# First expert weights in pairs, a last batch joined in halves, and inner blocks in two transfers

## The chip, the cores and the metric

The kernel runs on one core of one Trainium2 chip. The metric is the device time of one execution in microseconds (us), lower is better; the time given is the median of several executions. Beside it stands one execution recorded by the hardware profiler, from which all rows below come.

The engines are called as in the profile: PE is the matrix engine (PEld its weight loads), DVE the vector engine, ACT the scalar engine, POOL the third elementwise engine, SP the engine that issues nearly all transfers (DMAs) between memory and the on-chip buffer. PSUM banks, eight of them, take the results of matmuls.

## What is computed

Three stages follow one another: attention with a window of 64 positions over 4 batches, 8 heads, 576 positions and 64 values per head; a soft mixture of 8 experts with 4 slots each; and a feed-forward layer with a gated activation.

```python
scores = q @ k.T / 8, masked to 0 <= i - j < 64          # per batch and head
x = softmax(scores) @ v                                   # then (2304, 512)
logits = x @ phi                                          # (2304, 32)
d = exp(logits - logits.max(0)); d /= d.sum(0) + 1e-9     # over all tokens
slot_input = d.T @ x                                      # (32, 512)
for e in range(8):                                        # 4 slots each
    slot_out[e] = relu(slot_input[e] @ w1[e]) @ w2[e]     # 512x1024, 1024x512
c = softmax(logits, axis=1); x = c @ slot_out
h = x @ w_in; out = (h / (1 + exp(-1.702 * h))) @ w_out   # 512x2048, 2048x512
```

`w_in` and `w_out` come in 64-bit floats and are narrowed on the chip; everything else is 32-bit.

## The kernel before

**Attention steps.** The loop over `i` in `range(ns)` has 18 steps: 16 units (a batch and a pair of heads) and two that collect the last 64 positions of the batches. In each step PE makes scores (`emit_s`, L331 and L346), transposes the probabilities of the step before (`emit_t`, L366), transposes finished outputs (`xt_step`, L419) and makes the products with the values (`emit_pv`, L381). All engines run this in the order in which the code is written; the schedule is by hand (`manual_schedule`). SP issues the queries and keys of step `i + 3` (`load_qk`, L244), the values of step `i + 2` (`load_v`, L258) and, by the table `W_AT`, some weights (`load_w`, L154 and L164): at steps 10 to 15 (`AHEAD`) before the values, at the others behind them. SP waits at each issue until the buffer is free, and for the oldest of eight transfers under way, so its queue is in order.

**Weights.** Each expert's first and second weights come in slices of 1 MB, 128 rows of 2048 numbers. `w1` has 16 slices, one transfer each; `w2` has 16 too, of which 14 already come in pairs of 2 MB (`w2p`, L154), one alone, and the last in three pieces (`PIECES`, L164). `plan` lists them in order: the 16 of `w1`, then those of `w2`; each `load_w(1)` takes the next. Eight buffers of a pair each hold them, and the first `w2` go to parts of the `arena` that the attention has left. Four blocks of `w_in` (`early_load`, L169) are loaded in the first two steps, 512 KB each, into `raws`.

**The running sum of the slots.** `slot_input` is summed batch by batch with a running maximum: `acc` holds the sum so far in four groups of 32 rows, `al` is the factor by which it shrinks when the maximum moves. `gather` does `acc = acc * al + psl` for batches 1 and 2. For batch 3 (the last) and the 64 last positions of every batch (the "tail") this happens behind the loop, in the join: `psl` (L510) is the product of batch 3, `pl` (L760) that of the tail, whose rows 0 to 63 hold columns 0 to 255 and rows 64 to 127 columns 256 to 511 (`HALVES`). ACT scales `acc` by `al3`, the product of both factors (L764); DVE adds `psl * al` (L772) and then `pl`, half by half (L782). PE multiplies by `i4s` (L784), which sums the four row groups and divides by the sum of exponentials; ACT and DVE copy the two halves of the result `psi`, which lie in one bank, to `siT` (L786). PE then runs the experts: `emit_w1` (L810, four rounds), `emit_w2` (L853, 14 slices), `next_w2` (L912) and `last_w2` (L920).

**Feed-forward.** The rest, from about 135 us, loops over 48 blocks (L1065) and loads blocks of `w_out` and `w_in` while it runs. The change doesn't touch its code, but for the place of the `w_in` blocks in memory.

Of the kernel before, what the change touches and what calls it, by code (L numbers as in the profile page):

```python
# [10 lines left out]
F32 = mybir.dt.float32  # L11
# [5 lines left out]
ALU = mybir.AluOpType  # L17
# [14 lines left out]
HALVES = (slice(0, 256), slice(256, 512))  # L32
LAST_CUT = (slice(0, 384), slice(384, 512))
PIECES = (slice(0, 2), slice(2, 3), slice(3, 4))
W_AT = {**{i: 1 for i in range(2, 17)}, 12: 0, 15: 2, 16: 2, 17: 1}
L_AT = 12
AHEAD = range(10, 16)

# [29 lines left out]
FP = 4  # L68

@with_exitstack  # L70
def attention_softmoe_ffn(
# [6 lines left out]
    w1: bass.AP,  # L78
    w2p: bass.AP,
    w2s: bass.AP,  # L80
    w_in: bass.AP,
    w_out: bass.AP,
    out: bass.AP,
# [56 lines left out]
        return mem(2048 * i, 2048).rearrange("p (a f) -> p a f", a=4)  # L140

    w1t, w2t = [], []
    plan = [(w1t, w1, i, None if i < N_E else i - N_E) for i in range(16)]
    plan += [(w2t, w2p, i, i if i < 7 else None) for i in (0, 2, 4, 6, 7, 9, 11, 13, 15)]
    plan.reverse()

    def load_w(n=1):
        for _ in range(n):
            if plan:
                lst, src, i, d = plan.pop()  # L150
                if src is w2p and i not in (6, 15):
                    t = wpair() if d is None else mem(2048 * d, 4096).rearrange(
                        "p (n a f) -> p n a f", n=2, a=4)
                    nc.sync.dma_start(  # L154
                        out=t.rearrange("p n a f -> p (n a f)"), in_=w2p[W2P.index(i)])
                    lst.extend([t[:, 0], t[:, 1]])
                    continue
                t = wslot() if d is None else dslot(d)
                v = (w2s[i // 15] if src is w2p else src[i]).rearrange("p (a f) -> p a f", a=4)
                if not plan:  # L160
                    t, v = [x.rearrange("p a f -> p (a f)").rearrange(
                        "p (c a f) -> p c a f", c=4, a=4) for x in (t, v)]
                for c in PIECES if not plan else (slice(0, 4),):
                    nc.sync.dma_start(out=t[:, c], in_=v[:, c])  # L164
                lst.append(t)


    def raw_load(raw, src):
        nc.sync.dma_start(out=raw.bitcast(I32), in_=src.bitcast(I32))  # L169
# [32 lines left out]
    def early_dst(n):  # L202
        return win_dst(n) if n < FP else wof[:, n - FP, :]

    def early_raw(n):
        return raws[n // 2].rearrange("p a f -> p (a f)")[:, 1024 * (n % 2):1024 * (n % 2) + 1024]

    def early_load(n):
        src = w_in[n] if n < FP else w_out[n - FP]
        if wide:  # L210
            raw_load(early_raw(n), src)
        else:
            nc.sync.dma_start(out=early_dst(n), in_=src)


    qkb = [rawt[:, 0:1024]] + [mem(QK0 + 1024 * i, 1024) for i in range(2)]
# [519 lines left out]
    nc.vector.tensor_tensor(out=al, in0=m, in1=run["m"], op=ALU.subtract)  # L736
    psl = slots()
    load_w(1)
    sides[0][0]()
    ss = sp.tile([128, 1], F32, tag="ss", name="ss")  # L740
    nc.scalar.activation(
# [6 lines left out]
        nc.tensor.transpose(pd[:, t, :], ltt[0:32, t * 128:t * 128 + 128], ident[0:32, 0:32])  # L748
    sr = sp.tile([128, 1], F32, tag="srun", name="srun")
    nc.vector.tensor_tensor(out=sr, in0=run["s"], in1=al, op=ALU.mult)  # L750
    al3 = sp.tile([128, 1], F32, tag="al3", name="al3")
    nc.vector.tensor_tensor(out=al3, in0=run["al"], in1=al, op=ALU.mult)
    nc.vector.tensor_copy(dt, pd)
    pm = bank("m")
    nc.tensor.matmul(pm[:, 0:1], i4m, sr, start=True, stop=True)
# [1 line left out]
    for c in range(2):  # L757
# [3 lines left out]
                pl[32 * g:32 * g + 32, HALVES[c]], dt[:, t, :], xl[:, t, HALVES[c]],  # L761
                start=True, stop=True, tile_position=(0, 32 * g))
    load_w(1)
    nc.scalar.activation(out=acc, in_=acc, func=ACTF.Copy, scale=al3)  # L764
    rsl = sp.tile([128, 1], F32, tag="rsl", name="rsl")
    nc.vector.tensor_scalar(
        out=rsl, in0=pm[:, 0:1], scalar1=ss, scalar2=1e-9, op0=ALU.add, op1=ALU.add)
# [1 line left out]
    i4s = cst.tile([128, NS], F32, name="i4s")  # L769
    nc.vector.tensor_scalar(  # L770
        out=i4s, in0=i4m[:, 0:NS], scalar1=rsl, scalar2=None, op0=ALU.mult)
    nc.vector.scalar_tensor_tensor(  # L772
        out=acc, in0=psl, scalar=al, in1=acc, op0=ALU.mult, op1=ALU.add)
    siT = phis
    sides[1][0]()
    for k in range(2):
        sides[k][1]()
    sides[2][0]()
    psi = bank("m", (128, KD, 32))
    for k, c in enumerate(HALVES):  # L780
        p = slice(64 * k, 64 * k + 64)
        nc.vector.tensor_tensor(out=acc[p, c], in0=pl[p, c], in1=acc[p, c], op=ALU.add)  # L782
        for kk in (2 * k, 2 * k + 1):
            nc.tensor.matmul(  # L784
                psi[:, kk, :], acc[:, kk * 128:kk * 128 + 128], i4s, start=True, stop=True)
        (nc.vector.tensor_copy if k else nc.scalar.copy)(  # L786
            siT[:, 2 * k:2 * k + 2], psi[:, 2 * k:2 * k + 2])
    sides[2][1]()
    ht = rawt
    nc.gpsimd.memset(ht[:, 0:LS0], 0.0)  # L790
# [99 lines left out]
    def win_more():  # L890
        n = FP + len(iraw)
        if n == NF:
            return
        if n % FP == 0:
            winf.append(gp.tile([128, 4, 512], F32, tag="wi", name="wi", bufs=2))
        iraw[n] = gp.tile([128, 1024], F32, tag="iraw", name="iraw", bufs=2)
        if wide:
            raw_load(iraw[n], w_in[n])
        else:
            nc.sync.dma_start(out=win_dst(n), in_=w_in[n])  # L900

    so = hsb[0]
    soT = rawt[:, 0:512].rearrange("p (k s) -> p k s", k=KD)
# [295 lines left out]
def _layout(q, k, v, moe_phi, moe_w1, moe_w2, moe2_w_in, moe2_w_out):  # L1199
    def units(a):  # L1200
        return a.reshape(B, NHP, 2, S, D)

    def words(a):
        return a.view(np.int64) if a.dtype == np.float64 else a

    order = np.concatenate(
        [np.arange(c * CH, c * CH + CH) for c in list(range(0, 8, 2)) + list(range(1, 8, 2))])
    qf = units(q).transpose(0, 1, 2, 4, 3).reshape(NU, 128, S)
    kf = units(k).transpose(0, 1, 2, 4, 3).reshape(NU, 128, S)
    vf = units(v).transpose(0, 1, 3, 2, 4).reshape(NU, S, 128)  # L1210
    qk = np.concatenate([qf[:, :, 0:512], kf[:, :, order]], axis=2)
    vt = vf[:, 0:512].reshape(NU, 4, 128, 128).transpose(0, 2, 1, 3)
    o7, e8 = slice(448, 512), slice(512, 576)
    sq = np.concatenate([qf[:, :, e8], kf[:, :, e8], kf[:, :, o7]], axis=2)
    sq = sq.reshape(B, NHP, 128, 192).transpose(0, 2, 1, 3).reshape(B, 128, 768)
    sv = np.concatenate([vf[:, e8], vf[:, o7]], axis=1)
    vt = np.concatenate([vt, sv.reshape(B, NHP, 128, 128).transpose(0, 2, 1, 3)], axis=0)
    one = np.zeros(vt.shape[:3] + (1,), vt.dtype)
    vt = np.concatenate([vt, one], axis=3).reshape(NU + B, 128, 516)
    vt = np.concatenate([one[:, :, 0], vt], axis=2)  # L1220
    ph = moe_phi.reshape(KD, 128, NS).transpose(1, 0, 2).reshape(128, KD * NS)
    w1 = moe_w1.reshape(2, 4, 4, 128, 2, 512).transpose(0, 4, 2, 3, 1, 5).reshape(16, 128, 2048)
    w2 = moe_w2.reshape(8, 2, 4, 128, 512).transpose(0, 1, 3, 2, 4).reshape(16, 128, 2048)
    last = w2[15:].reshape(1, 128, 4, 4, 128).transpose(0, 1, 3, 2, 4).reshape(1, 128, 2048)
    w2p = np.stack([np.concatenate([w2[i], w2[i + 1]], axis=1) for i in W2P])
    w2s = np.stack([w2[6], last[0]])
    wi = moe2_w_in.reshape(4, 128, 4, 512).transpose(2, 0, 1, 3).reshape(16, 128, 512)
    wo = moe2_w_out.reshape(16, 128, 512)
    return {"qk": qk, "vt": vt, "sq": sq, "phi": ph, "w1": w1, "w2p": w2p, "w2s": w2s,
            "w_in": words(np.ascontiguousarray(wi)), "w_out": words(np.ascontiguousarray(wo))}  # L1230


# [22 lines left out]
```

## Time and profile before

| | us |
|---|---|
| median of 3 executions | 362.58 (362.48 to 362.71) |
| the profiled execution | 362.39 |
| its span | 360.6 |
| PE busy in it | 351.1 (97%) |
| PE weight loads busy | 270.0 (75%) |
| DVE busy | 242.0 (67%) |
| ACT busy | 195.3 (54%) |

The span runs from the first to the last instruction; the time of the execution has a little more around it. The granted PE clock is at full speed in all 40 slices of the page. A chain of waits is followed back from the last instruction: each piece is work or a transfer that the next one waited for, and "issue" is time in which an engine waited for nothing that the profile shows. A transfer has a time of issue and a time from issue to landing; transfers that wait behind others show it in the second.

### The profile page before, as it was taken

Reading aid. Unit: us, or ns where it says so; the run is one execution under the profiler, and the core shown is the slowest. Engines: PE = TensorE matmul, PEld = TensorE weight load, DVE = VectorE, ACT = ScalarE, POOL = GpSimd, SP = SyncE. Lnnn points to the kernel's source line nnn. Section 1 sums busy time; section 2 is a strip of 40 time slices with the busy share of each in tenths; the row PEclk is TensorE's granted clock in tenths of the full one; section 3 lists DMA queues with packets and bytes.
Section 4 is the critical chain, followed back from the end, with each engine's and each line's share of the span. In section 5 each row is a group of like instructions: output and inputs, shape, how many; then the busy total and the mean of one; then the engine's idle time right before and its main releaser. Section 6 shows DMA issues by size and latency. Waiting matters only on the chain.

```text
span 360.6 us, 7721 instructions
## 1 busy us (share of the span) xinstructions
PE 351.1 (97%) x3021; PEld 270.0 (75%) x3021; DVE 242.0 (67%) x527; ACT 195.3 (54%) x499; POOL 45.4 (13%) x90
## 2 busy tenths in 40 slices
PE   7999999998999999999999999999999999999995
PEld 6787787776634357888788887788886888888884
DVE  3767797986626328885867695988687876262624
ACT  2898899777314027765657444554445453333330
POOL 4366764630100000000000000000000000000000
PEclk9999999999999999999999999999999999999999
DMA  7999999999999994333131313040300000040404
GB/s 275 410 414 403 410 410 412 400 400 411 413 423 429 421 399 136 109 123 111 60 116 55 121 58 117 32 143 2 116 2 0 0 2 1 0 176 0 175 2 175
DMA packets 17172, 70.87 MB, mean 197 GB/s; under 512 B 1904, under 2 KB 2288, under 8 KB 14064
## 3 DMA queue, kind: packets, MB, share of 16 engines
q1 hardware_dynamic: 16992, 70.18, 50.3%
q8 instruction: 24, 0.39, 0.5%
q10 hardware_dynamic: 144, 0.20, 0.2%
q14 instruction: 12, 0.10, 0.1%
HBM read 65.65 MB, written 4.72 MB: 195 GB/s over the span
## 4 chain that ended last, share of the span: by engine, by line
PE 93%; DVE 3%; ACT 1%; issue 1%; DMA 1%; DVEq 0%; ACTq 0%
PE s L1065 18%; PE t L1065 18%; PE v L1065 18%; PE v L381 5%; PE m L1033 5%; PE s L346 5%; PE m L366 4%; PE s L810 4%; PE v L853 3%; PE s L331 2%; PE m L419 2%; PE m L460 1%; PE m L510 1%; DVE nm L351 1%; DMA rawt<-in_qk_dram 1%
## 5 line engine op out<-in xcount | busy, mean ns | idle before, releaser
L1021 ACT ACTIVATE r<-m 128x384 fp32r<-128x384 f32 (+1 forms) x97 | 47.4, 491 | 80.7 <-PE m L1033 80.6
L1046 DVE TENSOR_TENSOR r<-g,r 128x384 fp32r<-128x384 f32 x96 | 51.4, 554 | 48.4 <-ACT g L1021 39.9
L1065 PE MATMUL t<-w,r 128*128 128x512 f32 x288 | 75.9, 395 | 0.0
L1065 PE MATMUL s<-w,r 128*128 128x512 f32 x288 | 74.3, 393 | 0.0
L1065 PE MATMUL v<-w,r 128*128 128x512 f32 (+2 forms) x291 | 73.4, 387 | 0.0
L1065 PEld LDWEIGHTS t<-w,r 128*128 128x128 f32 x288 | 53.8, 188 | 14.8 <-issue 4.0
L1065 PEld LDWEIGHTS v<-w,r 128*128 128x128 f32 x291 | 54.5, 188 | 11.3
L1065 PEld LDWEIGHTS s<-w,r 128*128 128x128 f32 x288 | 52.6, 188 | 8.5
L1021 ACT ACTIVATE g<-m 128x384 f32<-128x384 f32 x96 | 47.8, 500 | 0.0
L358 ACT ACTIVATE pa<-s,nm 128x128 f32<-128x128 f32 x140 | 40.9, 404 | 5.7 <-DVE nm L351 5.7
L351 DVE TENSOR_REDUCE nm<-s 128x4 f32<-128x512 f32 x35 | 22.5, 684 | 5.4 <-PE s L346 4.9
L1033 PE MATMUL m<-cT,w 128*128 128x384 f32 (+2 forms) x113 | 25.9, 320 | 0.0
L1033 PEld LDWEIGHTS m<-cT,w 128*128 128x128 f32 x113 | 20.8, 188 | 4.9 <-ACT g L1021 0.7
L366 PE MATMUL m<-ident,pa 128*128 128x128 f32 x144 | 20.9, 283 | 0.4 <-issue 0.2
L366 PEld LDWEIGHTS m<-ident,pa 128*128 128x128 f32 x144 | 15.6, 140 | 4.6 <-issue 1.7
L367 ACT COPY pa<-m 128x512 f32<-128x512 f32 x18 | 10.7, 596 | 10.3 <-PE m L366 10.3
L1001 ACT CAST w<-wf 128x512 fp32r<-128x512 f32 x15 | 9.4, 623 | 9.3 <-DVE wf L194 9.3
L810 PE MATMUL s<-w,phis 128*32 128x512 f32 x128 | 14.1, 594 | 0.0
L346 PE MATMUL s<-arena 64*64 64x128 f32 x352 | 13.8, 271 | 0.3 <-DVE arena L254 0.2
L400 DVE TENSOR_TENSOR arena<-v,rs 128x256 f32<-128x256 f32 x36 | 13.6, 419 | 0.6
L1004 DVE TENSOR_TENSOR w<-wf,w 128x512 fp32r<-128x512 f32 x15 | 10.3, 689 | 5.2 <-ACT w L1001 5.1
L1085 DVE TENSOR_TENSOR w<-s,w 128x512 f32<-128x512 f32 x18 | 11.6, 684 | 2.8 <-PE s L1065 2.8
(218 smaller groups left out, 454.4 us busy)
## 6 DMA issues: line engine op xcount, KB each, us to landing
w<-in_w_dram SPq DMA_DIRECT2D x16, 1024.0 KB, 9.4
w<-in_w_out_dram SPq DMA_DIRECT2D x16, 512.0 KB, 3.4
w<-in_w2p_dram SPq DMA_DIRECT2D x4, 2048.0 KB, 16.2
arena<-in_w2p_dram SPq DMA_DIRECT2D x3, 2048.0 KB, 10.5
iraw<-in_w_in_dram SPq DMA_DIRECT2D x12, 512.0 KB, 3.3
arena<-in_qk_dram SPq DMA_DIRECT2D x10, 512.0 KB, 9.0
out_dram<-w SPq DMA_DIRECT2D x16, 256.0 KB, 2.1
arena<-in_vt_dram SPq DMA_DIRECT2D x13, 258.5 KB, 7.3
```

Of the source, the lines that this page charges most:

```text
L346: nc.tensor.matmul(st[h][rows[j], c, :], q, k, start=False, stop=(c == 3), tile_position=(64 * h, 64 * j))
L351: nc.vector.tensor_reduce(out=nm[:, h], in_=st[h], axis=AX.X, op=ALU.max, negate=True)
L358: nc.scalar.activation(out=pb[h][:, c, :], in_=st[h][:, c, :], func=ACTF.Exp, bias=nm[:, h, c:c + 1], scale=1.0)
L366: nc.tensor.transpose(tt[:, c, :], pb[h][:, c, :], ident)
L381: nc.tensor.matmul(pvt[i][h][64 * j:64 * j + 64, c, :], ab[h][:, c, 64 * j:64 * j + 64], v, start=True, stop=True, tile_position=(0, 64 * j))
L400: nc.vector.tensor_tensor(out=o, in0=pv[h][:, :, 1 - h:65 - h], in1=rs[:, h].unsqueeze(2).to_broadcast([128, 4, 64]), op=ALU.mult)
L810: nc.tensor.matmul(ph[32 * j:32 * j + 32, :], siT[:, kk, :], w1t[4 * r + kk][:, j, :], start=(kk == 0), stop=(kk == KD - 1), tile_position ...
L1021: nc.scalar.activation(out=(gh, g)[part][:, a:e], in_=ph[:, a:e], func=ACTF.Gelu_apprx_sigmoid)
L1033: nc.tensor.matmul(ph[:, c - a:e - a], mst[:, f * 128:f * 128 + 128], cT(c, e - c), start=True, stop=True)
L1046: nc.vector.tensor_tensor(out=gl, in0=g, in1=gh.bitcast(F32), op=ALU.subtract)
L1065: nc.tensor.matmul(accs[t][:, h], a[:, c], b[:, h], start=(first and k == 0), stop=(last and k == 2 and h.stop == 512))
L1085: nc.vector.tensor_tensor(out=o[:, h], in0=accs[t][:, h], in1=o[:, h], op=ALU.add)
```

## The change

Four edits:

- `w1` is laid out in pairs of slices, as `w2` is, so that each transfer brings 2 MB, 128 rows of 4096 numbers. `W_AT` now names nine steps: a pair at 3, 5, 7, 9, 11, 14, 15, 16 and 17 (the one at 17 is the first of `w2`).
- The four inner blocks of `w_in` that are loaded early come in two transfers of 1 MB (`w_two`).
- In the join, `acc * al + psl` of batch 3 is done like that of the batches before, in two halves of the columns (`join`), as soon as `psl` is there. Behind it ACT scales only those quarters of `acc` to which DVE doesn't add the tail, and DVE scales the others as it adds (`acc * al + pl`). `al3` is gone.
- The two halves of `psi` lie in banks of their own.

```diff
-W_AT = {**{i: 1 for i in range(2, 17)}, 12: 0, 15: 2, 16: 2, 17: 1}
+W_AT = {i: 1 for i in (3, 5, 7, 9, 11, 14, 15, 16, 17)}
...
-    plan = [(w1t, w1, i, None if i < N_E else i - N_E) for i in range(16)]
+    plan = [(w1t, w1, i, None) for i in range(0, 16, 2)]
...
-                if src is w2p and i not in (6, 15):
+                if src is w1 or i not in (6, 15):
...
-                        out=t.rearrange("p n a f -> p (n a f)"), in_=w2p[W2P.index(i)])
+                        out=t.rearrange("p n a f -> p (n a f)"), in_=w1[i // 2] if src is w1 else w2p[W2P.index(i)])
...
     def early_load(n):
-        src = w_in[n] if n < FP else w_out[n - FP]
+        if n < FP:
+            if n % 2:
+                return
+            src = w_two[n // 2]
+            raw, o = raws[n // 2], winf[0][:, n:n + 2]
+            raw, o = [x.rearrange("p a f -> p (a f)") for x in (raw, o)]
+        else:
+            src, raw, o = w_out[n - FP], early_raw(n), early_dst(n)
...
     psl = slots()
     load_w(1)
+
+    def join(c):
+        nc.vector.scalar_tensor_tensor(
+            out=acc[:, c], in0=acc[:, c], scalar=run["al"], in1=psl[:, c], op0=ALU.mult, op1=ALU.add)
+
+    join(HALVES[0])
     sides[0][0]()
...
     nc.vector.tensor_tensor(out=sr, in0=run["s"], in1=al, op=ALU.mult)
-    al3 = sp.tile([128, 1], F32, tag="al3", name="al3")
-    nc.vector.tensor_tensor(out=al3, in0=run["al"], in1=al, op=ALU.mult)
+    join(HALVES[1])
     nc.vector.tensor_copy(dt, pd)
...
-    nc.scalar.activation(out=acc, in_=acc, func=ACTF.Copy, scale=al3)
+    for k, c in enumerate(HALVES):
+        q = slice(64 - 64 * k, 128 - 64 * k)
+        nc.scalar.activation(out=acc[q, c], in_=acc[q, c], func=ACTF.Copy, scale=al[q])
...
-    nc.vector.scalar_tensor_tensor(
-        out=acc, in0=psl, scalar=al, in1=acc, op0=ALU.mult, op1=ALU.add)
...
-    psi = bank("m", (128, KD, 32))
+    psi = [bank("m")[:, 0:64].rearrange("p (k s) -> p k s", k=2) for _ in range(2)]
     for k, c in enumerate(HALVES):
         p = slice(64 * k, 64 * k + 64)
-        nc.vector.tensor_tensor(out=acc[p, c], in0=pl[p, c], in1=acc[p, c], op=ALU.add)
+        nc.vector.scalar_tensor_tensor(
+            out=acc[p, c], in0=acc[p, c], scalar=al[p], in1=pl[p, c], op0=ALU.mult, op1=ALU.add)
         for kk in (2 * k, 2 * k + 1):
             nc.tensor.matmul(
-                psi[:, kk, :], acc[:, kk * 128:kk * 128 + 128], i4s, start=True, stop=True)
+                psi[k][:, kk % 2], acc[:, kk * 128:kk * 128 + 128], i4s, start=True, stop=True)
         (nc.vector.tensor_copy if k else nc.scalar.copy)(
-            siT[:, 2 * k:2 * k + 2], psi[:, 2 * k:2 * k + 2])
+            siT[:, 2 * k:2 * k + 2], psi[k])
```

What stands in SP's queue from the end of step 1 to step 5 (`in_qk` the queries and keys, `in_vt` the values, `in_w` the first weights), before:

```order
L244 DMA arena<-in_qk_dram 128x1024
L258 DMA arena<-in_vt_dram 128x517
L164 DMA w<-in_w_dram 128x2048
L244 DMA rawt<-in_qk_dram 128x1024
L258 DMA arena<-in_vt_dram 128x517
L164 DMA w<-in_w_dram 128x2048
L244 DMA arena<-in_qk_dram 128x1024
L258 DMA rawt<-in_vt_dram 128x517
L164 DMA w<-in_w_dram 128x2048
```

and after:

```order
L252 DMA arena<-in_qk_dram 128x1024
L266 DMA arena<-in_vt_dram 128x517
L252 DMA rawt<-in_qk_dram 128x1024
L266 DMA arena<-in_vt_dram 128x517
L155 DMA w<-in_w_dram 128x4096
L252 DMA arena<-in_qk_dram 128x1024
L266 DMA rawt<-in_vt_dram 128x517
```

Each weight transfer of an even step has gone, and that of the odd step behind it is twice as long.

DVE in the join, from the difference of the maxima (`al`) to the second half of the sum, before (`m` and `v` are the banks of `psl` and `pl`, `srun` the sum of exponentials):

```order
L736 TENSOR_TENSOR al<-mrun 128x1
L750 TENSOR_TENSOR srun<-srun,al 128x1
L752 TENSOR_TENSOR al_1880<-al 128x1
L753 COPY rawt<-m 128x64
L766 TENSOR_SCALAR rsl<-m,ss 128x1
L768 RECIPROCAL rsl<-rsl 128x1
L770 TENSOR_SCALAR i4s<-i_82,rsl 128x32
L772 SCALAR_TENSOR_TENSOR acc<-m,al,acc 128x512
L782 TENSOR_TENSOR acc<-v,acc 64x256 x2
```

and after:

```order
L744 TENSOR_TENSOR al<-mrun 128x1
L749 SCALAR_TENSOR_TENSOR acc<-acc,al,m 128x256
L764 TENSOR_TENSOR srun<-srun,al 128x1
L749 SCALAR_TENSOR_TENSOR acc<-acc,al,m 128x256
L766 COPY rawt<-m 128x64
L781 TENSOR_SCALAR rsl<-m,ss 128x1
L783 RECIPROCAL rsl<-rsl 128x1
L785 TENSOR_SCALAR i4s<-i_82,rsl 128x32
L795 SCALAR_TENSOR_TENSOR acc<-acc,al,v 64x256 x2
```

The update of 512 columns behind `i4s` has become two of 256 columns, ahead of the copy of `pd` (L753 before, L766 after).

## Rows read from the trace of the kernel before

**Rows 1.** The page: DMA engines' load in 40 slices; instruction queue, packets and MB.
```profile
DMA  7999999999999994333131313040300000040404
...
q8 instruction: 24, 0.39, 0.5%
```

**Rows 2.** Chain of waits, 84 to 136 us: start, length, what.
```profile
88.80 1.43 issue
...
95.31 0.59 PE s L565 x4
...
97.18 0.67 DVE acc L772
...
97.94 0.43 DVE acc L782
...
99.08 0.22 ACT phis L786
```

**Rows 3.** Chain of waits, 0 to 85 us.
```profile
0.74 3.29 DMA rawt<-in_qk_dram
...
81.73 0.18 issue
```

**Rows 4.** Instruction queue, packets begun, MB, share: 87.7:87.8, 79.4:79.5 and 16:60 us.
```profile
q8 instruction: 1, 0.02, 67.9%
...
q8 instruction: 1, 0.02, 68.8%
...
q8 instruction: 7, 0.11, 1.1%
```

**Rows 5.** Timeline of PEld, 127.4 to 131.2 us: start, length, what, idle before.
```profile
127.44 0.13 PEld L853 LDWEIGHTS v<-w,rawt 128*32 128x32 f32 x4 [0.30 <-issue]
128.07 0.35 PEld L853 LDWEIGHTS v<-w,rawt 128*32 128x32 f32 x8 [0.51 <-DMA w<-in_w2p_dram]
...
130.70 0.16 PEld L920 LDWEIGHTS v<-w,rawt 128*32 128x32 f32 x8
```

**Rows 6.** Line L154 from 101.8 to 107.1 us: four issues, first and last landing.
```profile
L154 SPq DMA_DIRECT2D w<-in_w2p_dram x4: 327/328/328, 101.9 to 107.0; - x4
...
DMA to landing us min/median/max: 11.4/16.2/21.0
```

**Rows 7.** Line L164 from 110.8 us: the last piece of second weights.
```profile
L164 SPq DMA_DIRECT2D w<-in_w2s_dram x1: 424/424/424, 110.8 to 110.8; - x1
...
DMA to landing us min/median/max: 19.8/19.8/19.8
```

**Rows 8.** Line L164 from 73.4 and from 81.0 us: two issues each.
```profile
L164 SPq DMA_DIRECT2D w<-in_w_dram x2: 425/820/1214, 73.5 to 74.8; - x2
...
DMA to landing us min/median/max: 8.9/9.5/10.1
...
L164 SPq DMA_DIRECT2D w<-in_w_dram x2: 373/398/422, 81.0 to 81.5; - x2
...
DMA to landing us min/median/max: 7.6/8.7/9.7
```

**Rows 9.** Line L258 at 65.6 us, then SP's timeline: the next issue.
```profile
L258 SPq DMA_DIRECT2D rawt<-in_vt_dram x1: 328/328/328, 65.6 to 65.6; - x1
...
DMA to landing us min/median/max: 8.7/8.7/8.7
...
68.47 0.33 SPq L246 DMA_DIRECT2D arena<-in_sq_dram  x1
```

**Rows 10.** Timelines of DVE and PE, 95 to 98.5 us.
```profile
95.61 0.16 DVE L750 TENSOR_TENSOR srun<-srun,al 128x1 f32<-128x1 f32 x1 [0.58 <-ACT al L743]
...
96.17 0.22 DVE L753 COPY rawt<-m 128x64 f32<-128x64 f32 x1 [0.33 <-PE m L748]
...
97.51 0.60 PE L565 MATMUL v<-ident,rawt 128*128 128x128 f32 x4
```

More of the change, by code (lines that the diff above doesn't have):

```diff
@@ L80, in attention_softmoe_ffn @@
     w2s: bass.AP,
+    w_two: bass.AP,
     w_in: bass.AP,
@@ L158, in load_w @@
                 t = wslot() if d is None else dslot(d)
-                v = (w2s[i // 15] if src is w2p else src[i]).rearrange("p (a f) -> p a f", a=4)
+                v = w2s[i // 15].rearrange("p (a f) -> p a f", a=4)
                 if not plan:
@@ L208, in early_load @@
     def early_load(n):
-        src = w_in[n] if n < FP else w_out[n - FP]
+        if n < FP:
[6 more added lines that the diff above has]
+            src, raw, o = w_out[n - FP], early_raw(n), early_dst(n)
         if wide:
-            raw_load(early_raw(n), src)
+            raw_load(raw, src)
         else:
-            nc.sync.dma_start(out=early_dst(n), in_=src)
+            nc.sync.dma_start(out=o, in_=src)
     qkb = [rawt[:, 0:1024]] + [mem(QK0 + 1024 * i, 1024) for i in range(2)]
@@ L897, in win_more @@
         if wide:
-            raw_load(iraw[n], w_in[n])
+            raw_load(iraw[n], w_in[n - FP])
         else:
-            nc.sync.dma_start(out=win_dst(n), in_=w_in[n])
+            nc.sync.dma_start(out=win_dst(n), in_=w_in[n - FP])
     so = hsb[0]
@@ L1221, in _layout @@
     ph = moe_phi.reshape(KD, 128, NS).transpose(1, 0, 2).reshape(128, KD * NS)
-    w1 = moe_w1.reshape(2, 4, 4, 128, 2, 512).transpose(0, 4, 2, 3, 1, 5).reshape(16, 128, 2048)
+    w1 = moe_w1.reshape(2, 4, 4, 128, 2, 512).transpose(0, 4, 2, 3, 1, 5).reshape(8, 2, 128, 2048)
+    w1 = w1.transpose(0, 2, 1, 3).reshape(8, 128, 4096)
     w2 = moe_w2.reshape(8, 2, 4, 128, 512).transpose(0, 1, 3, 2, 4).reshape(16, 128, 2048)
@@ L1227, in _layout @@
     wi = moe2_w_in.reshape(4, 128, 4, 512).transpose(2, 0, 1, 3).reshape(16, 128, 512)
+    two = wi[:4].reshape(2, 2, 128, 512).transpose(0, 2, 1, 3).reshape(2, 128, 1024)
     wo = moe2_w_out.reshape(16, 128, 512)
     return {"qk": qk, "vt": vt, "sq": sq, "phi": ph, "w1": w1, "w2p": w2p, "w2s": w2s,
-            "w_in": words(np.ascontiguousarray(wi)), "w_out": words(np.ascontiguousarray(wo))}
+            "w_two": words(np.ascontiguousarray(two)),
+            "w_in": words(np.ascontiguousarray(wi[4:])), "w_out": words(np.ascontiguousarray(wo))}
 def kernel(**inputs):
```

## The prediction

> **What bounds the kernel now.** I read the page first: TensorE (PE) is busy for 351.1 of 360.6 us, and the DMA engines are at full load from the second slice of 9 us to about 135 us, after which their row falls to a third [rows 1]. All edited code runs before that point, so I read only the stretch to 136 us. Behind it the feed-forward loop is PE work from end to end, and what the first part gains or loses is carried to the end unchanged.
>
> Next the chain of waits of the first part, for what stands in it beside PE. In the join of the last batch (95 to 100 us) it has vector (DVE) pieces, the longest 0.67 (L772) and 0.43 us (L782), and between two PE pieces a scalar (ACT) copy of 0.22 us [rows 2]. In the attention steps the only pieces that are not work are called "issue"; the two that matter are 0.18 us at 81.73 and 1.43 us at 88.80 [rows 2, 3].
>
> What are they? The page counts 24 packets of 0.39 MB on an instruction queue [rows 1]; with 2 x 3021 PE instructions that is one packet of 16 KB for each 252 of them. One starts between 87.7 and 87.8 us and takes 67.9% of 16 x 0.1 us, 1.09 us, so it ends at 88.8 to 88.9 [rows 4]; PE stops at 88.80 and goes on at 90.23 [rows 2]. Another starts at 79.4 to 79.5, takes 1.10 us, ends near 80.6 [rows 4], and PE goes on at 81.91 [rows 3]. Both times PE resumes 1.3 to 1.4 us after the packet's end. So I read these stops, 1.61 us together, as PE waiting for its next block of instructions, which comes through the same DMA engines as the data.
>
> Last, who waits for whom at the end of the experts. Weight loads in L853 usually have 0.30 us before them; at 128.07 it is 0.51, ended by a transfer of second weights [rows 5], issued at 107.0 and landed 21.0 us later, at 128.0 [rows 6]. The very last piece is issued at 110.8 and lands after 19.8 us, at 130.6 [rows 7]; the loads that use it start at 130.70 [rows 5]. So at 128 us the transfers are late by 0.51 - 0.30 = **0.21 us**, and at 130.7 they are just in time. **PE and DMA are level there: a gain must shorten both.**
>
> **The change part by part.**
>
> *Transfers.* Sixteen 1 MB transfers become eight of 2 MB, four of 512 KB two of 1 MB; the bytes are the same. Two 1 MB transfers issued at 73.5 and 74.8 land at 82.4 and 84.9, 2.5 us apart; two more, from 81.0 and 81.5, at 88.6 and 91.2 [rows 8]. Four of 2 MB land from 113.3 to 128.0, (128.0 - 113.3)/3 = 4.9 apart [rows 6]. A pair saves 2 x 2.5 - 4.9 = 0.1, eight of them 0.8 us. The two inner pairs are half as large and have smaller rows to begin with; I give them 0.1 each, between nothing and 0.2: together **1.0 us**. The rows are rounded to 0.1, so a pair of first weights may save nothing or 0.2: bounds 0 and 2.0.
>
> [...]
>
> *Does the saving reach 130.6?* Only if the queue never runs dry. Steps 2, 4, 6, 8, 10 and 13 now issue no weights, so for a while up to 2.5 us of work is missing from it. The place to look is step 14. Before, the value transfer issued at 65.6 lands 8.7 us later, at 74.3 [rows 9]; with one slice less ahead of it (2.5) and the saving of five pairs and two inner ones (0.7) it lands at 71.1, while the next transfer is issued at 68.47 [rows 9] and a pair right behind it: 2.6 us. The first transfer of the program, on an idle queue, lands 3.29 us after its issue [rows 3], of which 512 KB at half of 2.5 are 1.3; so 2.0 us are needed before data flows. It just holds; if not, some tenths are lost. First weights now arrive later within the attention, but the last of them lands at 91.2 [rows 8], and they are used only after 99.3 [rows 2].
>
> *Nothing else in the attention lands later.* After every step the weights issued are as many as before or 1 MB fewer (even steps and 13), and step 14's pair stands ahead of the values as its single slice did. Queries, keys and values come at the same time or up to 2.5 us earlier. SP issues eight loads and two inner ones less, so nothing new queues there.
>
> *The join.* The 128x512 update (L772, 0.67 in the chain) goes from its place behind i4s. Two 128x256 updates stand earlier; for each I take 0.43, from the 64x256 piece of L782 [rows 2], since partitions run side by side; bounds 0.34 (half of 0.67) and 0.5. The first now waits for the products of L510, which end at 95.31, where the next PE piece begins [rows 2]; it fills a gap of 0.58 us on DVE [rows 10]: 95.35 to 95.78. Queued behind it: L750 (0.16, to 95.96; PE wants its result at 96.1), the second half (to 96.40) and the copy L753 of 0.22, which ended at 96.39 [rows 10] and now ends at 96.6. L760 on PE reads this copy, so it and the transposes behind it slip by 0.22 us: that is the price. In exchange i4s, which ended at 97.18 [rows 2], ends near 97.4 and the last update (0.43) follows it at once, to 97.85. PE ends its transposes at 97.51 + 0.60 + 0.22 = 98.33 [rows 10] and starts L784 there, not at 98.41: 0.08 gained. The second half of L784 has a bank of its own and needs no ACT copy before it: 99.06 to 99.34, 0.28, goes. Together **0.35 us**; bounds 0.1 (the copy slips by 0.47) and 0.6 (it doesn't slip). ACT's scaling in two 64x256 pieces now waits for the second half and holds the casts behind it for some 0.3 us; PE's transposes (to 98.33) cover that, and without them it would cost the 0.3. The removed al3 is DVE time only.
>
> *Instruction blocks.* No PE instruction is added or removed. Blocks share the engines with data, and the queue is shorter in six steps. No row shows when a block was asked for, so the effect is bounded by all 1.61 us going and, above, by the second rival. I take at least 0.45 us of relief: the stop at 88.80 alone is 1.43, and step 13 before it has one slice less.
>
> **Sum.** PE: 0.21 + 0.35 = 0.56, with 0.45 of relief 1.01. DMA: 1.0. The smaller counts: 1.0. The profiled execution took 362.39 us (span 360.6), so 361.4; against the median of 362.58, 0.19 above it, **361.6**.
>
> **The rivals.**
>
> *PE alone (24%).* The instruction stops stay; the gain is 0.56: 362.0. For it: nothing in the rows proves that a shorter data queue brings blocks sooner. Against: both blocks of [rows 4] arrive under full DMA load.
>
> *Blocks behind pairs (15%, slower).* If a block must let the transfer under way pass, that is 4.9 instead of 2.5 us, 2.4 more. Pairs fill 8 x 4.9 = 39 of the 71 us from 20 to 91, so half of some eleven blocks (7 of them from 16 to 60 us [rows 4]) meet one. Five hits at half of 2.4 are 6.0 us; with two lost in slack 3.6 remain: 362.58 - 0.56 + 3.6 = 365.6. It decides from 0.56 us of new stops on. Against it: from 101 to 128 us, with 2 MB transfers only, the chain has no stop, though PE uses its instructions more slowly there.
>
> [...]
>
> *Transfers save nothing (9%).* Then the last piece still lands at 130.6 and the time is 362.5. The rounding of the rows allows it; against it stand the two equal distances of 2.5 and the mean of three for 4.9.
>
> **How the numbers follow.** Forecast 361.6 at 52%, with a range of its own of 361.3 to 361.9 (1.3 saved, or 0.3 lost to a dry queue). Range 361.3 to 363.6: it takes in the forecast, the first and the third rival and the mild end of the second, and leaves out some 13%. A difference under 0.2% (0.73 us, about what a measurement of this kernel can tell from none) counts as the same. Below 361.85 lies nine tenths of the forecast and a fifth of the first rival, 0.52; above 363.3 most of the second, 0.14; the rest is 0.34.
>
> **What would show it.** The last piece lands near 129.6, and the loads that use it start within 0.1 us of that. Pairs of first weights land 4.9 us after what stands ahead of them. L784 has no gap in its middle. The issue stops sum to under 1.2 us where these two made 1.61, and no new ones come. It is wrong if the stops grow, if L853 and L920 no longer wait for transfers that land at 129.6 (PE bound), or if the DMA row shows holes before 90 us.

## The result and the profile after

The changed kernel takes **368.36 us** in the median of six executions (364.21 to 370.43) against 362.63 (362.48 to 362.99) of the kernel before beside it: ratio 1.0116, 95% interval 1.0086 to 1.0146. It is slower by 1.2% in this ratio and by 1.6% in the medians; forecast were 361.6 us and a range that ended at 363.6. The profiled execution took 368.2 us (span 366.4). One thing is needed to read what follows: executions of one kernel spread on these chips (the kernel before took 361.9 to 369.8 us in 144 executions, 47 of them above 365), so medians and shares above 365 us are given over all executions, and the ratios leave out those over 1.5% above the fastest of their kernel.

The page of the changed kernel, the rows that answer to [rows 1]: TensorE clock, DMA load and GB/s in 40 slices of 9.2 us, and the instruction queue.

```profile
PEclk9999999789999999999999999999999999999999
DMA  7999999699999996324131505031300000040404
GB/s 281 415 404 411 405 408 412 232 366 403 405 404 433 429 402 247 114 77 154 37 93 43 172 2 173 1 120 54 114 2 0 0 2 0 1 174 0 172 2 173
...
q8 instruction: 24, 0.39, 0.4%
```

The unbroken row of nines up to 135 us has a hole in the eighth slice, at 64 to 73 us: 232 GB/s where its neighbours have 412 and 366. In the same slice and the next the row PEclk has 7 and 8 where all others have 9. The chain of waits there (start, length, what):

```profile
65.15 1.21 PE m L468 x32
66.36 0.34 PE s L339 x4
66.70 0.43 PE s L354 x15
67.13 2.92 issue
70.05 1.32 PE s L354 x17
71.37 1.90 PE m L374 x8
73.27 0.85 PE m L427 x4
74.12 1.93 PE v L389 x32
76.06 0.57 PE m L497 x2
76.63 0.34 PE s L339 x4
76.97 0.87 PE s L354 x32
77.84 1.02 PE m L374 x8
```

PE stops in the middle of the scores of step 14 (L354, the old L346) for **2.92 us**; at that place before stood 0.13 us:

```profile
67.51 0.13 issue
```

What comes next runs at half pace: eight transposes of L374 take 1.90 us, six microseconds later 1.02. The windows show the granted clock (third column from the end), the share of the DMA engines and GB/s:

```profile
65.00:70.00 5.00, 2.13 (x57) 1.29 (x53) 2.39 (x10) 2.28 (x9) 2.67 (x7) 0.96 0.84 321
70.00:75.00 5.00, 4.95 (x47) 4.29 (x49) 2.72 (x7) 2.28 (x8) 2.32 (x7) 0.50 0.53 181
75.00:80.00 5.00, 5.00 (x78) 3.57 (x74) 3.27 (x11) 3.41 (x12) 0.17 (x1) 0.86 0.97 402
```

After the stop the granted clock is 0.50 for the whole of 70 to 75 us; in the kernel before it was 1.00 there. Is the stop an instruction block, as read in [rows 2 to 4]? The instruction queue from 67.4 to 67.5 us (packets begun, MB, share of 16 engines in 0.1 us):

```profile
q8 instruction: 1, 0.02, 64.8%
```

64.8% of 1.6 us is 1.04, so this block ends at 68.5 and PE goes on 1.6 us later. In the kernel before it began at 65.25. In all 20 profiles of this study PE has 82 such stops over 0.1 us before 140 us; every one ends 1.21 to 1.66 us after the end of a block's packet, and every one falls on the 193rd or 194th PE instruction (weight loads and PE's waits counted) above a multiple of 256.

SP's issues tell where the DMA hole is from (start, length of the issue, line, what):

```profile
65.25 0.33 SPq L266 DMA_DIRECT2D rawt<-in_vt_dram  x1
71.45 0.33 SPq L254 DMA_DIRECT2D arena<-in_sq_dram  x1
72.19 0.33 SPq L155 DMA_DIRECT2D w<-in_w_dram  x1
```

For 6.2 us nothing is issued: these loads wait until PE has freed their buffers (the first one 5.8 us for L354), and the pair of step 14 stands behind them. The values issued at 65.25 land at 70.81, and then the queue is empty. At the end, the weight loads that answer to [rows 5] (start, length, idle before and what ended it):

```profile
133.54 0.16 PEld L867 LDWEIGHTS v<-w,rawt 128*32 128x32 f32 x8 [2.08 <-DMA w<-in_w2p_dram]
...
136.11 0.16 PEld L934 LDWEIGHTS v<-w,rawt 128*32 128x32 f32 x8 [0.25 <-DMA w<-in_w2s_dram]
```

PE waits there 2.08 us where it was 0.51, and the last piece comes at 136.07, not 130.65. The feed-forward loop (L1079, the old L1065) starts at 141.25 where it was 135.98: 5.3 us later, nearly all of the 5.8 between the two profiled executions.

The join alone does what it should, and more:

```profile
99.20 1.04 PE m L518 x8
...
100.26 0.48 DVE acc L749
100.74 0.07 DVE srun L764
100.81 0.39 DVE acc L749
101.21 0.14 DVE rawt L766
...
103.06 0.81 PE m L798 x8
103.87 2.26 PE s L824 x17
```

From the end of L518 to the experts' first product it takes 103.87 - 100.24 = 3.63 us. Before, L510 ended at 95.31 and L810 began at 99.97, 4.66 us later; the sums there (L784) took two runs with ACT's copy between them:

```profile
98.41 0.65 PE m L784 x4
...
99.97 3.12 PE s L810 x25
```

### The profile page after: what moved, and what is told of

Read it like the earlier page. It is cut to its first block, busy times and chain, and to the rows that moved or that the text cites. A ratio compares the mean times of both kernels' runs of the same rounds, so it can differ in the third digit from the quotient of the medians.

```text
span 366.4 us, 7715 instructions
## 1 busy us (share of the span) xinstructions
PE 353.0 (96%) x3021; PEld 271.5 (74%) x3021; DVE 241.3 (66%) x527; ACT 195.9 (53%) x500; POOL 44.3 (12%) x90
## 4 chain that ended last, share of the span: by engine, by line
PE 88%; DMA 7%; issue 2%; DVE 1%; ACT 0%; DVEq 0%; ACTq 0%
PE s L1079 18%; PE t L1079 18%; PE v L1079 18%; DMA w<-in_w2p_dram 6%; PE v L389 5%; PE m L374 5%; PE m L1047 5%; PE s L354 5%; PE m L427 2%; PE s L339 2%; PE s L824 2%; PE m L468 1%; PE m L518 1%; DMA rawt<-in_qk_dram 1%; PE m L961 1%
## 5 line engine op out<-in xcount | busy, mean ns | idle before, releaser
L1079 PE MATMUL t<-w,r 128*128 128x512 f32 x288 | 75.9, 395 | 0.0
L1079 PE MATMUL s<-w,r 128*128 128x512 f32 x288 | 74.3, 392 | 0.0
L1079 PE MATMUL v<-w,r 128*128 128x512 f32 (+2 forms) x291 | 73.5, 388 | 0.0
L1079 PEld LDWEIGHTS t<-w,r 128*128 128x128 f32 x288 | 53.8, 188 | 14.8 <-issue 4.0
L1079 PEld LDWEIGHTS v<-w,r 128*128 128x128 f32 x291 | 54.5, 188 | 11.4
L1079 PEld LDWEIGHTS s<-w,r 128*128 128x128 f32 x288 | 52.6, 188 | 8.5
L374 PE MATMUL m<-ident,pa 128*128 128x128 f32 x144 | 21.9, 291 | 0.7 <-issue 0.4
L374 PEld LDWEIGHTS m<-ident,pa 128*128 128x128 f32 x144 | 16.4, 145 | 5.3 <-issue 2.1
L354 PE MATMUL s<-arena 64*64 64x128 f32 x352 | 14.6, 279 | 2.9 <-issue 2.9
L354 PEld LDWEIGHTS s<-arena 64*64 64x64 f32 x352 | 11.8, 137 | 4.1 <-issue 3.4
```

Source lines behind the costliest of these rows:

```text
L354: nc.tensor.matmul(st[h][rows[j], c, :], q, k, start=False, stop=(c == 3), tile_position=(64 * h, 64 * j))
L374: nc.tensor.transpose(tt[:, c, :], pb[h][:, c, :], ident)
L1079: nc.tensor.matmul(accs[t][:, h], a[:, c], b[:, h], start=(first and k == 0), stop=(last and k == 2 and h.stop == 512))
```

## The experiments

The theory after this reading, called A in the expectations: blocks wait behind the 2 MB pairs; a late block stops PE; the clock falls; and since SP's loads wait for PE, the data queue runs dry, so that the last weights are late. The rivals: the schedule does it, not the transfers (B); the join or the inner blocks (C); the clock falls for a reason of its own (D). All times of the experiments, with what was run on the chips beside them:

| kernel | executions | median us | above 365 us | ratio to before, 95% |
|---|---|---|---|---|
| before | 144 | 363.30 | 47 | |
| changed | 26 | 367.61 | 19 | 1.0116 (1.0086 to 1.0146); 1.0081 (1.0035 to 1.0127); 1.0043 (0.9993 to 1.0093) |
| pairs alone (e2) | 10 | 367.08 | 9 | 1.0075 (1.0043 to 1.0106) |
| pairs as two transfers (e3, e11, e15) | 30 | 366.14 | 20 | 1.0054 (1.0022 to 1.0086); 1.0028 (0.9981 to 1.0075); 1.0042 (1.0005 to 1.0079) |
| one pair (e7, e16) | 20 | 364.78 | 10 | 1.0020 (0.9980 to 1.0059); 0.9988 (0.9938 to 1.0038) |
| no pairs (e1, e12, e17) | 34 | 363.17 | 7 | 0.9966 (0.9926 to 1.0005); 0.9966 (0.9930 to 1.0003); 1.0006 (0.9962 to 1.0050) |
| no pairs, even (e9, e18) | 24 | 362.79 | 1 | 0.9979 (0.9940 to 1.0017); 0.9964 (0.9929 to 0.9999) |

**Which part does the harm? No pairs (e1), pairs alone (e2).**

```diff
 e1: the changed kernel with
-W_AT = {i: 1 for i in (3, 5, 7, 9, 11, 14, 15, 16, 17)}
+W_AT = {**{i: 1 for i in range(2, 17)}, 12: 0, 15: 2, 16: 2, 17: 1}
-    plan = [(w1t, w1, i, None) for i in range(0, 16, 2)]
+    plan = [(w1t, w1, i, None if i < N_E else i - N_E) for i in range(16)]
 e2: the kernel before with the opposite edit, and nothing else
```

> The changed kernel with the first weights as sixteen single slices at the old steps; the join in halves and the inner blocks in two transfers stay. Theory A (an instruction block has to wait behind a 2 MB pair, PE stops for 2.9 us near 67 us, its clock falls, the loads go out late): no stop above 1.5 us, granted clock 1.00 in every stretch to 140 us, 362.1 us (361.8 to 362.6). Rival C (the join or the inner transfers did the harm): 366 us or more.

> The kernel before with the pairs of first weights alone, at the steps of the changed kernel; join and inner blocks as before. Theory A: one stop of 2 to 3 us between 60 and 75 us, granted clock under 0.8 in the ten microseconds after it, 366 to 369 us. Rival C (the pairs are harmless by themselves): 361.5 to 363 us.

Without pairs: median 362.60, stops as before (the longest 1.43 us), clock 1.00 throughout. Pairs alone: 367.08. Rival C falls; the pairs do it. The stops in the chain of e2:

```profile
62.89 0.89 issue
69.40 2.37 issue
...
85.87 1.01 issue
```

and its windows behind the long one:

```profile
70.00:75.00 5.00, 3.22 (x61) 2.82 (x61) 3.00 (x9) 1.79 (x7) 4.07 (x11) 1.00 0.41 136
75.00:80.00 5.00, 4.92 (x70) 3.15 (x68) 4.13 (x12) 4.52 (x16) 1.22 (x2) 1.00 1.01 416
```

Here A missed one thing: the clock stays at 1.00, and yet the queue is as empty, 136 GB/s. The lower clock is not needed for the loss.

**What does a stop cost by itself? (e4)**

```diff
         for c in range(4):
+            if i == 14 and c == 2:
+                for _ in range(5):
+                    nc.gpsimd.tensor_scalar(
+                        out=qbuf(u)[:, 128:512], in0=qbuf(u)[:, 128:512],
+                        scalar1=1.0, scalar2=1.0, op0=ALU.mult, op1=ALU.mult)
```

> The kernel before with one stop put into PE at the place where the changed kernel stops: in the middle of the scores of step 14, five GpSimd operations that multiply the queries by 1.0 hold PE for about 3 us. Theory A (the stop itself brings the lower clock, and both delay the loads): granted clock under 0.8 in the ten microseconds behind it, the first feed-forward matmul 4 to 7 us later than before, 366 to 370 us. Rival D (the stop costs its own length and no more; the lower clock has another cause): clock 1.00, at most 365.6 us.

368.98 us (367.05 to 370.05, four executions), ratio 1.0141 (1.0091 to 1.0191). GpSimd began later than I had reckoned, so the stop is 4.26 us (PE's timeline; in brackets the idle time before and what ended it). Then the window 70 to 75 us:

```profile
72.30 1.13 PE L351 MATMUL s<-arena 64*64 64x128 f32 x16 [4.26 <-POOL arena L337]
```
```profile
70.00:75.00 5.00, 2.70 (x24) 2.37 (x25) 1.50 (x4) 0.43 (x1) 4.44 (x11) 0.62 0.36 123
```

A stop of PE alone, with no change to any transfer, brings both the lower clock (0.62) and the empty queue (123 GB/s). Rival D's bound on the time was set for a stop of 3 us, so the time does not refute it; the clock and the empty queue do. The rest of the loss follows from the stop.

**Do the stops come from data traffic at all? (e10)**

```diff
                 lst, src, i, d = plan.pop()
+                if src is w1 and i > 1:
+                    lst.append(lst[i % 2])
+                    continue
```

> The kernel before with only the first two of the sixteen slices of first weights loaded; all experts use these two in turn, so 14 MB are not read. This leaves the attention with a data queue that is not full. Theory A (PE's stops are blocks that wait behind data): blocks start less than 3 us after PE has used up the one before where it was 5.3 us on average, no instruction stop above 0.15 us before 100 us, 359.5 to 360.8 us. Rival H (the stops belong to the sequence of instructions itself): stops of about 1.98 us in all remain, 361.5 us or more.

The kernel leaves out 14 of the 16 first slices, so its time does not compare: 359.06 us (358.47 to 359.48), 0.9851 of before (0.9789 to 0.9913). What counts are its stops. The page:

```profile
DMA  8997668538999993331321313130200000040404
GB/s 283 409 415 289 169 172 247 159 98 288 354 431 430 407 357 124 117 121 59 95 84 59 119 59 118 60 119 26 92 2 0 0 2 0 1 178 0 176 2 176
```

From 27 to 89 us the queue is not full. A single stop of 0.25 us is left, at 29 us, where the queue has only just emptied; behind it the chain has none: the longest "issue" piece from 60 to 92 us is 0.08. No row shows when a block is asked for. I count from the 150th PE instruction of each 256, since the earliest that any block of the 20 profiles starts is the 152nd, behind 200 us, where little data moves. So counted, the second to twelfth block start after 2.9 us on average (5.3 before). Rival H falls: with less data on the engines the blocks are in time.

**The size of the rows, or that two slices stand together? Two transfers for each pair (e3, e11, e15), 4 KB rows (e5).**

```diff
 e3, e11, e15: the changed kernel, single slices, two at a step
+W_AT = {i: 2 for i in (3, 5, 7, 9, 11, 14, 15, 16)}
+W_AT[17] = 1
 e5: as e1, each slice in two transfers
+HALF = (slice(0, 2), slice(2, 4))
-                for c in PIECES if not plan else (slice(0, 4),):
+                for c in PIECES if not plan else HALF if src is w1 else (slice(0, 4),):
```

> The changed kernel with two slices at each of the same steps, but as two 1 MB transfers with 8 KB rows instead of one of 2 MB with 16 KB rows. Theory A (the size of the rows holds the blocks up): stops no longer than the 1.43 us of the kernel before, clock 1.00, 362 to 363 us. Rival B (the schedule does it: bunches behind each other and steps without weights): the stop of about 2.9 us near 67 us and the lower clock stay, 366 to 369 us.

> The two slices at a step as two 1 MB transfers with 8 KB rows once more, for a second profile and more runs. Theory B2 (bunching, not the size of the rows): most runs 2 us or more above the kernel before, median 364.5 to 367 us. Theory A (the rows): median within 1 us of the kernel without pairs.

> Two slices at a step as two 1 MB transfers, for a third profile: theory B2, 365 to 367 us; theory A (the rows), within 1 us of the kernel before.

> As the kernel without pairs (single slices at the old steps, join in halves, two inner transfers), but each slice of first weights in two transfers of 512 KB, whose rows are 4 KB instead of 8. Theory A (a block waits the longer, the larger the rows that are queued ahead of it): the block that PE waits 1.43 us for near 90 us comes at least 1 us earlier, the instruction stops sum to under 0.8 us where they were 1.98; the transfers cost some 0.06 us per slice more, 1 us in all, so 361.5 to 363 us on a chip where the kernel before takes 362.5. Rival E (the delay of a block depends on what PE and the queue do, not on the rows): stops within 0.4 us of 1.98.

The three profiles of the split kernel have 0.12, 2.92 and 2.65 us at the place in step 14; its medians are 366.26, 365.75 and 366.02. The second one:

```profile
67.84 0.43 PE s L355 x15
68.27 2.92 issue
71.19 0.76 PE s L355 x17
```

So rows of 8 KB make the same stop. Nor do 4 KB rows help: the stop near 90 us is 1.70 instead of 1.43, all stops sum to 2.69 us, and the median is 363.77 (1.0016; 0.9978 to 1.0054). The 0.06 us per slice in that forecast was an estimate that no run shows; from 5 to 125 us e5 moved 401 GB/s, and e17, with rows of 8 KB, 412. Large rows are not needed for the loss; both forecasts of A missed here.

**Once more the changed kernel (e6, e14), and its sixth pair at step 13 (e8).**

> The changed kernel as it is, once more, for a second profile of it beside the runs of this call. Theory A: again a stop of 2 us or more between 60 and 75 us at a block's boundary, and an idle data queue behind it; whether the clock falls as well may differ from execution to execution. 365 to 370 us.

> The changed kernel, for a third profile beside the split one of the same chip. Theory B2: median within 1 us of the split kernel. Theory A (the rows add to it): 1.5 us or more above the split kernel.

> The changed kernel with the sixth pair at step 13 instead of 14. Theory A2 (the stop is paid twice: PE stands, and the data queue, which step 13 does not feed, runs dry behind it): the idle time of the data engines between 68 and 75 us falls from some 4 to under 1.5 us and the end comes 1.5 to 4 us earlier than in the changed kernel, 363.5 to 366 us. Rival G (the queue runs dry because every load behind the stop waits for PE, whatever is queued): idle time within 1 us of before, 366 to 370 us.

Medians 367.1 and 366.76 (the ratio of e14 is not clear of 1); both profiled executions (364.86 and 364.85) happened to have no long stop in step 14, against A's forecast for e6, so it does not come every time. Of the 20 profiled executions of the study, the eight with a stop of 2.3 us or more in step 14 (that of e4 among them) took 367.23 to 369.96 us, the other twelve at most 365.57. No execution of the kernel before above 365 us was profiled, so whether its 47 held such a stop is not known. e6 and e14 show what the pairs cost without it. The window 5 to 125 us, first of before, then of e17 (no pairs), then of e14 (all pairs):

```profile
5.00:125.00 120.00, 116.34 (x1887) 80.69 (x1891) 82.51 (x231) 79.81 (x240) 42.81 (x76) 1.00 1.02 410
```
```profile
5.00:125.00 120.00, 116.82 (x1899) 80.72 (x1903) 81.01 (x231) 80.09 (x241) 43.00 (x76) 1.00 1.02 412
```
```profile
5.00:125.00 120.00, 115.65 (x1883) 80.97 (x1887) 80.60 (x230) 80.25 (x241) 42.95 (x76) 1.00 1.01 404
```

404 is 1.5% under 410: over 120 us that is 1.8 us (e6 has 405). The last piece of weights lands at 132.75 in e14, at 130.65 before.

With the pair at step 13 (`W_AT` with 13 for 14) the median is 365.44, the ratio 1.0011 (0.9964 to 1.0057). The profiled execution took 368.88: from 60 us on it has stops of 0.99, 2.65 and 2.29 us, with the clock at 1.00 after the second. In its 70 to 75 us window, where PE stood, the engines moved 423 GB/s: here a filled queue carried over the stop. But they fell to 247 in the next five, so the hole is put off and made smaller, not closed: from 65 to 85 us 7.5 MB moved, against 6.1 in the changed kernel and 8.0 before. A2's mechanism shows; that the end comes earlier does not, in this profile. The median lies in A2's range, but the interval overlaps that of e6 on the same chip (1.0035 to 1.0127).

**One pair (e7, e16) and its split form (e13).**

```diff
 e7, e16: before, slices 8 and 9 as one 2 MB transfer at step 11, none at step 10
 e13: before, the same two as 1 MB transfers at step 11
+W_AT = {**{i: 1 for i in range(2, 17)}, 10: 0, 11: 2, 12: 0, 15: 2, 16: 2, 17: 1}
```

> The kernel before with one pair only: the slices of steps 10 and 11 become one 2 MB transfer at step 11; everything else is as before. Theory A with one guilty pair (the block that is asked for near 61 us waits behind this pair): a stop of 1.5 us or more near 68 to 71 us, an idle data queue behind it, 364.5 to 369 us. Rival F (it takes the whole row of pairs, each leaving less lead for the next block): stops within 0.5 us of before, 362 to 363 us.

> The kernel before with the slice of step 10 issued at step 11, right ahead of that step's own: two 1 MB transfers with 8 KB rows one behind the other, nothing else changed. Theory B2 (bunching): as with the one 2 MB pair at this place, part of the executions have the stop of some 2.9 us near 70 us; the block that is asked for near 61 us starts 7 us later or more, where it was 4.2; median 364 to 366 us. Theory A (rows of 16 KB): that block after 4 to 5 us, stop of 0.1 to 0.3 us, median within 0.5 us of the kernel before.

> The kernel before with the one 2 MB pair at step 11, for a second profile beside its split form: theory B2, median within 0.7 us of the split form; theory A, 1 us or more above it.

With the pair, both profiles have the stop in step 14, 2.92 us each. In the split form it is 0.12. The chain of e16, then that of e13:

```profile
68.44 2.92 issue
```
```profile
67.39 0.12 issue
```

The block in question began at 68.8 us in e16 and at 65.1 in e13. Medians on that chip: 364.95 and 362.64, but the ratios 0.9988 (0.9938 to 1.0038) and 1.0011 (0.9960 to 1.0061) do not part them, nor do 5 and 4 executions of 10 above 365 us. So the long stop comes with one pair too, where rival F had stops within 0.5 us of before. In this single place the form with small rows did better, against what bunching alone would give: its block came after 4.1 us and the medians are 2.31 us apart, both as A forecast. For all eight pairs e14 and e15 on one chip are alike (366.76 and 366.02), as B2 forecast. **That the larger rows add something is neither shown nor excluded.**

**The rest of the change by itself (e12, e17), and spread evenly (e9, e18).**

```diff
 e9, e18: as e1, one slice at every step
-W_AT = {**{i: 1 for i in range(2, 17)}, 12: 0, 15: 2, 16: 2, 17: 1}
+W_AT = {**{i: 1 for i in range(2, 17)}, 17: 2}
```

> The kernel with the join in halves and the two inner transfers alone once more, in more runs: 0.2 to 0.6 us under the kernel before, as the join's terms say (0.35 us); if the join is worth nothing, within 0.1 us of it.

> The join in halves and the two inner transfers with single slices at the old steps, a third time, in as many runs as can be had: 0.2 to 0.6% under the kernel before if the two earlier comparisons (0.9966 each) hold; within 0.1% if they were the spread of the runs.

> As the kernel without pairs (single slices, join in halves, two inner transfers), but the slices are spread evenly: one at every step from 2 to 16, also at step 12, and two transfers at step 17, where before steps 15 and 16 had two slices each and step 12 none. Theory B2 (a block of instructions waits for the data that is queued ahead of it, in whatever transfers, so that bunching makes the stops): the block that PE waits 1.43 us for near 90 us comes earlier, that stop falls under 0.8 us; the time is 0.3 to 1.0 us less than that of the kernel without pairs if the data queue stays full, and the same if it does not. Rival (the stop at 90 us has nothing to do with the slices at 15 and 16): 1.2 us or more remain.

> The same with the slices spread evenly over steps 2 to 17: 0.1 to 0.6% under the kernel before, and within 0.2% of the kernel with the old steps; the stop near 90 us stays at 1.4 us.

Join and inner transfers with the old steps: 0.9966, 0.9966 and 1.0006, each interval with 1 in it; the forecast for e17 missed, and a gain is not shown. Spread evenly: 0.9979 and 0.9964, the last with an interval that ends at 0.9999 (0.4% from e17, forecast at most 0.2%), and only one of 24 executions above 365 us. By this share it is the best version of the study that loads all weights: 0.2 and 0.4% ahead of before in the two comparisons, of which only the second is clear of 1, and 1.3% ahead of the changed kernel (362.79 against 367.61, over all chips). Its chain from 60 us:

```profile
88.94 1.43 issue
106.19 21.56 DMA w<-in_w2p_dram
```

and its weight loads:

```profile
127.80 0.16 PEld L867 LDWEIGHTS v<-w,rawt 128*32 128x32 f32 x8 [1.07 <-DMA w<-in_w2p_dram]
```

The stop near 90 us is 1.43 us to the hundredth, with less queued ahead of it: that forecast missed, and why it is so constant is not settled. The last row says where the join's gain is: PE now comes earlier and waits 1.07 us for weights, before 0.51 [rows 5].

## Why the prediction was wrong

**The bound: right.** PE and DMA are level at 128 us, and a gain must shorten both. e17 and e18 show it from the other side: of the 1.0 us by which the join is shorter, half is waited away at L867 (1.00 in e17 and 1.07 in e18, against 0.51).

**Instruction blocks: this step failed.** The stops were read rightly as PE waiting for 16 KB blocks that come among the data: the stops end 1.21 to 1.66 us after a block's packet, and in e10, with 159 to 247 GB/s around it, the block of step 14 starts 1.3 us after its reckoned request and not 3.5 to 8. But the term had the wrong sign: "at least 0.45 us of relief", where the stops over 0.1 us grew from 1.98 to 5.22 us in the profiled executions. The argument was that the queue is shorter in six steps. The block of step 14 came some 2.2 us later all the same, at 67.43. How much is queued when it is asked for does not explain that: from the reckoned request on, the transfers already issued take 8.1 us to land in the changed kernel and 8.4 before, yet 2.75 MB pass ahead of the block where 1.66 MB did.

What the profiles show instead are two delays. Without e10, this block starts 3.5 to 4.3 us after its reckoned request in twelve of them, behind 1.4 to 1.7 MB, and 6.9 to 8.1 us after it in seven, behind 2.7 to 3.3 MB; none lies between. The seven are among the eleven that bring two slices at once ahead of it, and none among the eight with single slices there. So bunched weights make the late block likelier; why it lets more data pass in one execution than in another stays open.

The second rival, "Blocks behind pairs", at 15%, had the outcome: blocks behind pairs come late, and the kernel is slower. Its reason, the size of the transfer under way, is not borne out, since two transfers of 1 MB make the same stop. I held against it that from 101 to 128 us the chain has no stop though only 2 MB transfers run. That was no evidence: blocks start there some 15 us apart (109.3, 124.1 and 138.7 in the changed kernel), in the attention 6 to 10, so a block can be late there and nobody waits. And its price, 365.6, was too low: it reckoned with five small hits, and one block made 2.92 of the 5.22 us.

**A stop was priced once, and is paid three times.** First PE stands: 2.92 us. Second, the lower clock behind it (0.50 from 70 to 75 us): the transposes, L427 and L389 take 1.90 + 0.85 + 1.93 us where the same work took 1.02 + 0.44 + 1.08 in the kernel before, 2.1 more. Third, the one that decides: SP's loads wait for PE, so the data queue, which has no slack to the end, loses bytes. The 10 us windows from 60 to 80 us, first of before, then of the changed kernel:

```profile
60.00:70.00 10.00, 9.87 (x206) 7.58 (x200) 8.14 (x24) 7.46 (x24) 5.54 (x10) 1.00 1.03 405
70.00:80.00 10.00, 9.93 (x190) 7.60 (x188) 8.33 (x25) 8.14 (x28) 4.41 (x9) 1.00 1.01 400
```
```profile
60.00:70.00 10.00, 7.13 (x167) 5.62 (x163) 6.41 (x21) 5.92 (x20) 5.75 (x10) 0.98 0.91 358
70.00:80.00 10.00, 9.95 (x119) 7.86 (x119) 5.99 (x18) 5.69 (x19) 2.49 (x7) 0.68 0.75 292
```

That is (405 - 358) x 10 + (400 - 292) x 10 = 1,550 KB too little, 3.8 us at 407 GB/s: most of the 5.3 us. The first two payments lie beside the third and do not add to it: PE ends L518 4.93 us later than it ended L510 and has 1.03 of that back behind the join, the last piece of weights lands 5.42 us later, and PE waits for it.

**"It just holds": the place was right, the step was not.** The prediction looked at step 14, put the landing of its value transfer at 71.1 us and the next issue at 68.47. The landing came at 70.81. The issue came at 71.45, since PE had stopped; no stop had been put into that sum. In e14, without the long stop, the issues came at 69.18 and 69.92, before the values landed at 73.49, and it did hold.

**Transfers: the sign was wrong.** The term was 1.0 us saved. The first five pairs land 4.93, 4.93, 5.55, 5.18 and 4.97 us after the transfer ahead of them; 2 x 2.5 would be 5.0, so the best give back 0.07 each, not 0.1, and two cost more than two single slices. Over the whole stretch the rate falls from 410 to 404 GB/s. The distance of 4.9 had been measured at 113 to 128 us, where nothing but pairs stands in the queue; between pairs and small transfers three of five kept it. Why the others took longer is open: in e14, whose fourth pair takes 6.61 us, the engines are as busy from 40 to 55 us (shares of 0.98 to 1.00) but move 357 to 373 GB/s.

**The join: right in kind, too small.** Forecast 0.35 us (bounds 0.1 to 0.6), measured 4.66 - 3.63 = 1.03. The halves took 0.48 and 0.39 us in the chain (0.43 was reckoned). A piece of 64 partitions did take as long as one of 128: before, 64x256 0.42 (L782) and 128x256 0.42 (L400); after, 64x256 0.48 (L795) and 128x256 0.48 (L749). L798 has no gap in its middle. Two other terms were mis-sized. The copy was to slip by 0.22 us; it ends 1.11 us after L518, where it had ended 1.08 after L510, a slip of 0.03, so the sums (L798) start 0.28 us earlier and not 0.08. And the sums with ACT's copy between them took 99.97 - 98.41 = 1.56 us; in one run they take 0.81, so 0.75 goes and not 0.28.

**The granted clock.** Not forecast. The granted clock was below 1.00 behind the four stops of 2.92 us (0.50, 0.63, 0.66 and 0.73 in 70 to 75 us) and behind that of 4.26 (0.62 in e4), but 1.00 behind 2.37 (e2); behind 2.65 it was 0.66 in e15 and 1.00 in e8. Near 90 us it fell behind 1.70 (e5, 0.66 in 90 to 100 us) and not behind 2.24 (e3). The length of the stop alone does not decide it.

## What to carry to other kernels

In this kernel the instruction block of step 14 started 3.5 to 8 us after its reckoned request where the data queue ran at 400 GB/s, and 1.3 us after it where it ran at 159 to 247; before transfers are bunched, look in the trace at which other queue has packets among theirs and how much lead these have. Price a stop of an engine not by its length but by what waits for its progress: here PE freed the buffers of a load queue without slack, the queue moved 1,550 KB less from 60 to 80 us, and the last piece of weights landed 5.42 us later. And where a margin of some tenths decides, one profile is one draw: the changed kernel's three had the long stop once.

## What the runs showed of the hardware

At all 82 stops in 20 profiles PE goes on 1.21 to 1.66 us after the packet of an instruction block of 16 KB has ended. With the data queue full at 400 GB/s, the block of step 14 starts 3.5 to 8 us after its reckoned request; in e10, with 159 to 247 GB/s around it, after 1.3. Between request and start pass 1.4 to 1.7 MB or 2.7 to 3.3 MB of data, in e10 0.4 MB. The page of the changed kernel counts 24 such packets, 0.39 MB together, on the instruction queue, and its profiled execution has 5.22 us of stops over 0.1 us.

The stop in step 14 has two sizes and nothing between: at most 0.22 us, or 2.37 to 2.92 (e4's own stop apart). What decides between them in an execution is open.
